# One token granule's second FFN matmul as seven half-size products, with two weight sums on GpSimd

## The chip, the cores and the metric

One NeuronCore of a Trainium2 chip runs the whole program. The metric is device time in microseconds of one execution; three runs of the kernel before gave 208.34, 208.65 and 208.99, with a median of 208.65. A separate, profiled execution gives the trace from which all durations below come.

## The reference

Attention with a local window and a few global keys is followed by a two-layer FFN with a squared ReLU:

```python
scores = scale * np.matmul(q, k.transpose(0, 1, 3, 2))   # q, k, v: (4, 8, 768, 64)
keep = is_global | is_local                               # 8 global keys, 96 local ones
scores = np.where(keep, scores + bias, -1e9)              # bias: -slope * distance
a = softmax(scores)
x = (a @ v).transpose(0, 2, 1, 3).reshape(3072, 512)
h = x @ w_in                                              # (512, 2048)
r = np.maximum(h, 0.0)
out = (s * (r * r) + b) @ w_out                           # (2048, 512), s and b scalars
```

Inputs and output are float32; matmuls run on bfloat16 operands and accumulate in float32.

## The kernel before, in words

Tokens are cut into 12 *granules* of 256 tokens (two blocks of 128), three to a batch; a granule's attention is four *units* of two heads each. For every unit the kernel computes scores on TensorE (`stage_S`, L444), exponentials on ScalarE (L453), a multiplication with a mask template on VectorE (L460), and the product with the values (`stage_A`, L504), whose result VectorE normalizes (a reciprocal L468, a multiplication L469). The granule's normalized rows are transposed into `xT` by DMAs of the SP queue (`x_by_dma`, L612). The first FFN matmul (`p1_mm`, L632) multiplies `xT` with `w_in`, two 128-wide slices of the 2048 at a time; ScalarE takes the ReLU (L642) and VectorE the square (L645), or ScalarE squares four slices at once (L808). The result `gT` holds g = r*r, transposed, for a pair of granules.

The second FFN matmul has two forms. Granules 0 to 3 use the plain one: `p2_mm` (L680) accumulates 16 matmuls of 128x512 for each block of 128 tokens, and VectorE finishes with s and the bias vector `bvec` (`p2_out`, L691; `p2_late`, L713, for the blocks of granules 0 and 1, which were held back until `bvec` existed). Granules 4 to 11 are taken in pairs: a pair's even and odd granule and the halves of the 2048 and of the 512 columns make a 2x2 block product, computed with seven half-size products (`product`, L832) instead of eight. That form needs sums of quarters of g (`g_sum`, L795), sums of the partial results (`scaled` L841, `join` with L880), and four weight matrices that are differences of quarters of `w_out` (w11 and w12 the upper half's left and right columns, w21 and w22 the lower half's): `weight_sums` at L766 to L769, where t1 = w12 - w11, t2 = w22 - t1, t3 = w22 - w12 and t4 = w21 - t2. t3 is written over w12 in the tile `w_out_bf`. Each is one VectorE instruction over 128x2048 elements.

The order of all work is written out by hand: every engine runs its instructions in the order in which the Python code issues them. From granule 4 on, `step(s, c0, c1, c2)` issues, in this order: the scores and exponentials of the next step, the masks of the next step, the list `c0`, `stage_A` of the first unit, a `flush()` of the waiting evacuations (`outs`), `c1`, `stage_A` of the second unit, another flush, and `c2`; at the end of a granule `finish_granule` issues the transposes of `xT` and, on POOL, a one-element copy out of `xT` (the *gate*, L122), behind which the loads of a later granule are queued. Steps 8 to 12 (L1167 to L1176) are the ones that change: they hold the rest of granule 2's and all of granule 3's second matmul, the first matmul of granules 3 and 4, and three of the four weight sums.

PSUM is shared by three pools; the pool `ps_h`, with three banks, serves the FFN of both kinds. SBUF work tiles of one tag and one buffer are reused, so a new user waits for the last reader of the old one.

Of the kernel before, what the change touches and what calls it, by code (L numbers as in the profile page):

```python
# [8 lines left out]
F32 = mybir.dt.float32  # L9
BF16 = mybir.dt.bfloat16  # L10
ACT = mybir.ActivationFunctionType
ALU = mybir.AluOpType
# [5 lines left out]
def kernel(  # L18
# [25 lines left out]
    KC = DM // P  # L44
    FC = DF // P
# [18 lines left out]
    ps_h = ctx.enter_context(tc.tile_pool(name="ps_h", bufs=3, space=bass.MemoryType.PSUM))  # L64
# [102 lines left out]
    s_bc = const.tile([P, 1], F32, name="s_bc")  # L167
    b_bc = const.tile([P, 1], F32, name="b_bc")

    def load_scalars():  # L170
# [23 lines left out]
        out=far, in0=far, scalar=NEG_BIG, in1=rel, op0=ALU.mult, op1=ALU.add  # L194
# [15 lines left out]
    for i in range(2, 4):  # L210
        load_w_in(i, 4)
    nc.gpsimd.affine_select(
        out=late_bf[:, 3, :],
# [411 lines left out]
    def p1_mm(j, fp):  # L625

        g = g_of(j)
        ps = ps_h.tile([P, 2, GT], F32, name="ps_1", tag="psh")
        for i in range(2):
            fc = 2 * fp + i  # L630
            for kc in range(KC):
                nc.tensor.matmul(  # L632
                    ps[:, i, :],
                    lhsT=w_in_bf[:, kc, fc * P : (fc + 1) * P],
                    rhs=xT[j][:, kc, :],
                    start=(kc == 0),
                    stop=(kc == KC - 1),
                )
        gs = g[:, 2 * fp : 2 * fp + 2, :]

        def relu():
            nc.scalar.activation(gs, ps[:], ACT.Relu)  # L642

        def square():
            nc.vector.tensor_tensor(gs, gs, gs, ALU.mult)  # L645

        return relu, square


    bvec = const.tile([P, DM], F32, name="bvec")  # L650
# [24 lines left out]
    def p2_mm(j, tb, lo=0, hi=FC):  # L675
        if lo == 0:
            po_cur[j, tb] = ps_h.tile([P, DM], F32, name="ps_2", tag="psh")
        po = po_cur[j, tb]
        for fc in range(lo, hi):
            nc.tensor.matmul(  # L680
                po[:],
                lhsT=g_of(j)[:, fc, tb * P : (tb + 1) * P],
                rhs=w_out_bf[:, fc, :],
                start=(fc == 0),
                stop=(fc == FC - 1),
            )
# [32 lines left out]
    outs = []  # L719
# [9 lines left out]
    def moe_p2_cols(j, tb, parts):  # L729
# [27 lines left out]
    NH = FC // 2  # L757
    CH = DM // 2
    w11, w12 = (w_out_bf[:, 0:NH, c * CH : (c + 1) * CH] for c in range(2))
    w21, w22 = (w_out_bf[:, NH:FC, c * CH : (c + 1) * CH] for c in range(2))  # L760
    t1, t2, t4 = (
        const.tile([P, NH, CH], BF16, name=f"wsub{i}", tag=f"wsub{i}")[:] for i in range(3)
    )
    t3 = w12
    weight_sums = [
        lambda: nc.vector.tensor_tensor(t1, w12, w11, ALU.subtract),  # L766
        lambda: nc.vector.tensor_tensor(t2, w22, t1, ALU.subtract),
        lambda: nc.vector.tensor_tensor(t3, w22, w12, ALU.subtract),
        lambda: nc.vector.tensor_tensor(t4, w21, t2, ALU.subtract),  # L769
    ]  # L770

    gs_cur = {}
# [5 lines left out]
    def g_sum(pr, n, c=None):  # L778

        def go():  # L780
            if pr not in gs_cur:
                gs_cur[pr] = [
                    gpool.tile([P, NH, GT], BF16, name="gsum", tag=f"gsum{i}", bufs=1)
                    for i in range(4)
                ]
            e, o = 2 * pr, 2 * pr + 1
            cs = slice(0, NH) if c is None else slice(c * NH // 2, (c + 1) * NH // 2)
            s1, s2, s3, s4 = (t[:, cs, :] for t in gs_cur[pr])
            dst, x, y, op = {
                1: (s1, quarter(o, 0, c), quarter(o, 1, c), ALU.add),  # L790
                2: (s2, s1, quarter(e, 0, c), ALU.subtract),
                3: (s3, quarter(e, 0, c), quarter(o, 0, c), ALU.subtract),
                4: (s4, quarter(e, 1, c), s2, ALU.subtract),
            }[n]
            nc.vector.tensor_tensor(dst, x, y, op)  # L795

        return go
# [42 lines left out]
    def scaled(dst, ps, add):  # L840
        nc.vector.scalar_tensor_tensor(  # L841
            out=dst, in0=ps, scalar=s_bc[:], in1=add, op0=ALU.mult, op1=ALU.add
        )

    bdiff = const.tile([P, CH], F32, name="bdiff")
# [33 lines left out]
    def add_f32(dst, x, y):  # L879
        nc.vector.tensor_tensor(dst, x, y, ALU.add)  # L880
# [27 lines left out]
    def join(pr, n):  # L908
# [11 lines left out]

        return go

    def pe(pr, n):

        def go():
            product(pr, n)
            outs.append(lambda: evac(pr, n))

        return go
# [4 lines left out]
    def u1(j, q):  # L934
        return lambda: unit_p1(j, q)

    def late_p1(j, fps):

        def go(fp):
            relu, square = p1_mm(j, fp)  # L940
            relu()
            outs.append(square)

        return [lambda fp=fp: go(fp) for fp in fps]

# [4 lines left out]
    def run(cs):  # L950
        for c in cs:
            c()
# [19 lines left out]
    def step(s, c0, c1, c2, pool=None, pre=()):  # L972

        j = 2 * s // HP
        last = (2 * s + 2) % HP == 0
        if not last and j >= 4 and j + 2 < NJ:
            qk_by_dma(j + 2)
        posts = scores(s + 1)
        exps, masks = [c for i, c in enumerate(posts) if i % 2 == 0], posts[1::2]
        run(exps)  # L980
        run(pre)
        run(masks)
        run(c0)
        stage_A(2 * s)
        flush()
        if not last and j + 1 == QK_PE + 1:
            make_koff(j + 1)
        if not last and j % NGR == 0:
            attach(j // NGR, 1, NB)
        run(c1)  # L990
        stage_A(2 * s + 1, pool)
        flush()
        n = 2 if j < X_PE else 1
        run(c2[0:n])
        if last:
# [167 lines left out]
    def rest(j, tb):  # L1163
        p2_mm(j, tb, FC // 2, FC)
        outs.append(lambda: p2_out(j, tb))

    step(8, [lambda: rest(2, 0)] + late_p1(3, (0,)), late_p1(3, (1, 2)), late_p1(3, (3,)))  # L1167
    step(9, p2[2][1:2], late_p1(3, (4, 5)), late_p1(3, (6, 7)))
    step(10, p2[3][0:1], [lambda: shifted_template(range(H))], late[0:2] + [bias_diff], ps_h)
    step(  # L1170
        11,
        [lambda: p2_mm(3, 1, 0, FC // 2), u1(4, 0)],
        [u1(4, 1)],
        late[2:4] + [shifted_copy, weight_sums[0]],
    )
    step(12, [lambda: rest(3, 1), u1(4, 2)], [weight_sums[1], u1(4, 3)], [weight_sums[2]])  # L1176
    for pr in range(2, NJ // 2):
        e, o = 2 * pr, 2 * pr + 1
        k0 = 2 * e + 5
        if k0 >= NU // 2:  # L1180
            break
        step(
            k0,
            [pe(pr, 2)],
            [u1(o, 0)],
            [u1(o, 1), flush, g_sum(pr, 3, 0)],
            pre=[pe(pr, 1), flush],
        )
        step(
            k0 + 1,  # L1190
            [u1(o, 2)],
            [u1(o, 3), g_sum(pr, 1, 0)],
            [g_sum(pr, 1, 1), pe(pr, 7), g_sum(pr, 2)] + [weight_sums[3]] * (pr == 2),
            pre=[g_sum(pr, 3, 1)],
        )
        tail = k0 + 3 >= NU // 2
        step(
            k0 + 2,
            [u1(e + 2, 0), pe(pr, 5)] if tail else [pe(pr, 5), flush, pe(pr, 6)],
            [pe(pr, 6), g_sum(pr, 4, 0)] if tail else [g_sum(pr, 4, 0), prod(pr, 4)],  # L1200
            [g_sum(pr, 4, 1), u1(e + 2, int(tail)), join(pr, 1)],
        )
# [66 lines left out]
```

The softmax here doesn't subtract the row's maximum and nothing guards it: scores larger than these inputs give would overflow.

## Time and profile before

| | us |
|---|---|
| median of 3 runs | 208.65 (208.34 to 208.99) |
| the profiled execution's own time | 208.38 |
| its span, first to last instruction | 206.6 |
| TensorE busy | 201.9 |
| VectorE busy | 160.9 |
| ScalarE busy | 127.8 |
| GpSimd (POOL) busy | 69.9, nearly all of it issuing DMAs |
| one weight sum on VectorE (L766 to L769) | 1.22 |
| second matmul of granule 3, block 0 (L680) | 76.97 to 80.44 |
| first use of granule 4's `xT` (L632) | 83.20 |

The profile's rows name an engine, a line of the kernel, an operation, what it writes and reads, and a duration. PE is TensorE, DVE VectorE, ACT ScalarE, POOL GpSimd, SP the queue that issues DMAs. Matmul durations overlap, so a stretch of matmuls is read from the start of the first to the start of what follows. POOL was idle from 70.3 to 82.96, waiting for granule 4's `xT`.

### The profile page before, as it was taken

How to read it: one execution, taken by the hardware profiler on the slowest of the kernel's cores; microseconds unless marked ns; L12 is line 12 of the kernel's file. 1: busy time of each engine (PE TensorE's matmuls, PEld its weight loads, DVE VectorE, ACT ScalarE, POOL GpSimd, SP SyncE). 2: the span in 40 equal slices, each digit the busy share in tenths (PEclk: the TensorE clock that was granted, in tenths of full speed). 3: DMA queues.
4: the chain of work that ended last, by engine and by line, in shares of the span. 5: the costliest groups of instructions: out<-in, count | busy, mean ns of one | idle time of the engine just before them, and what ended most of it. 6: DMA issues, size and time to landing. Idle time of an engine off the chain costs nothing.

```text
span 206.6 us, 5313 instructions
## 1 busy us (share of the span) xinstructions
PE 201.9 (98%) x2182; PEld 160.1 (77%) x2190; DVE 160.9 (78%) x338; ACT 127.8 (62%) x197; POOL 69.9 (34%) x90
## 2 busy tenths in 40 slices
PE   8999999999999999999999999999999999999993
PEld 2678884557867585878888898888888889888883
DVE  7977589977989866799799975699866696737974
ACT  5766669486976558685664595663695764476200
POOL 8986333899454500913700907300000000000000
PEclk9999999999999999999999999999999999999999
DMA  5999999999999999999999999999570300240006
GB/s 163 173 179 201 207 206 178 156 153 130 130 147 119 156 121 218 208 195 214 148 205 149 116 125 212 167 219 77 53 206 3 98 9 0 61 145 0 0 10 197
DMA packets 110836, 28.17 MB, mean 136 GB/s; under 512 B 97852, under 2 KB 109308, under 8 KB 110812
## 3 DMA queue, kind: packets, MB, share of 16 engines
q0 software_dynamic: 76000, 13.11, 85.9%
q1 hardware_dynamic: 33612, 14.13, 41.0%
q10 hardware_dynamic: 1200, 0.59, 1.1%
q8 instruction: 17, 0.28, 0.6%
q14 instruction: 7, 0.06, 0.1%
HBM read 27.26 MB, written 6.29 MB: 162 GB/s over the span
## 4 chain that ended last, share of the span: by engine, by line
PE 95%; DMA 2%; DVE 1%; issue 0%; ACT 0%
PE ps L632 41%; PE ps L832 24%; PE ps L680 13%; PE ps_s L444 6%; PE ps_av L504 5%; DMA first<-in_k_dram 2%; PE ps_s L530 1%; PE ps_t L354 1%; PE ps_x L604 1%; PE ps_t L331 1%; PE ps_s L545 1%; PE ps_s L419 1%; PE ps_av L571 1%; PE ps_last L832 0%; PE ps_t L344 0%
## 5 line engine op out<-in xcount | busy, mean ns | idle before, releaser
L632 PE MATMUL ps<-xT,w_in_bf 128*128 128x256 bf16 x768 | 90.4, 273 | 0.1
L642 ACT ACTIVATE gT<-ps 128x512 bf16<-128x512 f32 x96 | 55.9, 598 | 47.9 <-PE ps L632 47.6
L632 PEld LDWEIGHTS <-w_in_bf 128*128 128x128 bf16 x768 | 73.1, 98 | 9.6 <-DVE xT L607 0.2
L453 ACT ACTIVATE pt<-ps_s 128x1024 bf16<-128x1024 f32 (+1 forms) x44 | 39.3, 946 | 3.2 <-PE ps_s L444 3.0
L680 PE MATMUL ps<-w_out_bf,gT 128*128 128x512 bf16 x120 | 28.7, 380 | 0.5 <-issue 0.2
L460 DVE TENSOR_TENSOR pt<-pt,tmpl 128x1024 bf16<-128x1024 bf16 (+1 forms) x40 | 24.4, 643 | 3.8 <-ACT pt L453 3.7
L832 PEld LDWEIGHTS <-gsum 128*128 128x128 bf16 x256 | 24.2, 98 | 3.7 <-DVE gsum L795 0.5
L108 POOL DMA_DIRECT2D vb<-in_v_dram x24 | 21.5, 910 | 5.5 <-DMA w_out_bf<-in_moe_w_out_dram 3.3
L806 DVE TENSOR_TENSOR gT<-gT 128x1024 bf16<-128x1024 bf16 x20 | 13.7, 686 | 11.7 <-ACT gT L642 11.7
L680 PEld LDWEIGHTS <-gT 128*128 128x128 bf16 x128 | 11.7, 98 | 13.0
L469 DVE TENSOR_TENSOR xn<-ps_av,rc 128x256 bf16<-128x256 f32 x48 | 20.4, 424 | 1.7
L832 PEld LDWEIGHTS <-gT 128*128 128x128 bf16 x200 | 18.6, 98 | 2.3
L468 DVE RECIPROCAL rc<-ps_av 128x4 f32<-128x4 f32 x48 | 8.5, 178 | 12.3 <-PE ps_av L504 10.8
L504 PEld LDWEIGHTS <-pt 128*128 128x128 bf16 x320 | 14.4, 97 | 2.7 <-DVE xn L469 0.7
L645 DVE TENSOR_TENSOR gT<-gT 128x512 bf16<-128x512 bf16 x32 | 13.0, 420 | 3.6 <-ACT gT L642 3.3
L504 PE MATMUL ps_av<-vb,pt 128*128 128x65 bf16 x208 | 15.3, 193 | 0.0
L832 PE MATMUL ps<-w_out_bf,gsum 128*128 128x256 bf16 x128 | 15.3, 273 | 0.0
L832 PE MATMUL ps<-wsub,gsum 128*128 128x256 bf16 x128 | 15.1, 273 | 0.0
L116 POOL DMA_DIRECT2D nat<-in_q_dram x14 | 12.4, 888 | 7.0 <-DMA vb<-in_v_dram 2.7
L122 POOL COPY gate<-xT 1x1 bf16<-1x1 bf16 x6 | 1.5, 250 | 37.1 <-DMA xT<-xn 37.1
L116 POOL DMA_DIRECT2D nat<-in_k_dram x14 | 12.4, 884 | 4.9 <-DMA w_in_bf<-in_moe_w_in_dram 2.4
L832 PE MATMUL ps<-w_out_bf,gT 128*128 128x256 bf16 x120 | 13.9, 273 | 0.0
(111 smaller groups left out, 230.5 us busy)
## 6 DMA issues: line engine op xcount, KB each, us to landing
out_dram<-o_q SPq DMA_DIRECT2D x15, 256.0 KB, 2.6
vb<-in_v_dram POOLq DMA_DIRECT2D x24, 128.0 KB, 8.8
nat<-in_k_dram POOLq DMA_DIRECT2D x22, 128.0 KB, 6.7
nat<-in_q_dram POOLq DMA_DIRECT2D x22, 128.0 KB, 6.9
w_out_bf<-in_moe_w_out_dram POOLq DMA_DIRECT2D x4, 512.0 KB, 16.2
w_in_bf<-in_moe_w_in_dram POOLq DMA_DIRECT2D x4, 256.0 KB, 7.5
w_in_bf<-in_moe_w_in_dram POOLq DMA_DIRECT2D x2, 512.0 KB, 11.2
out_dram<-o_sb SPq DMA_DIRECT2D x4, 256.0 KB, 6.1
```

The costliest lines, as they stand in the source:

```text
L108: nc.gpsimd.dma_start(vbuf[b % 2][:, sb, :, 0:D], rows_of(v, b, sb))
L116: nc.gpsimd.dma_start(t[:, n, i, :, :], rows_of(srcs[n], b, sb))
L453: nc.scalar.activation(pt[:, :, 0:ncol], ps[:, :, 0:ncol], ACT.Exp, scale=QSCALE)
L460: nc.vector.tensor_tensor(pv, pv, m.rearrange("p h a c -> p h (a c)"), ALU.mult)
L469: nc.vector.tensor_tensor(dst, av[:, :, :, 0:D], rc[:].to_broadcast((P, 2, 2, D)), ALU.mult)
L504: nc.tensor.matmul(av[:, i, hi, 0 : D + 1], lhsT=pt[:, hi, c * P : (c + 1) * P], rhs=vv, start=(n == 0), stop=(n == len(terms) - 1),)
L632: nc.tensor.matmul(ps[:, i, :], lhsT=w_in_bf[:, kc, fc * P : (fc + 1) * P], rhs=xT[j][:, kc, :], start=(kc == 0), stop=(kc == KC - 1),)
L642: nc.scalar.activation(gs, ps[:], ACT.Relu)
L645: nc.vector.tensor_tensor(gs, gs, gs, ALU.mult)
L680: nc.tensor.matmul(po[:], lhsT=g_of(j)[:, fc, tb * P : (tb + 1) * P], rhs=w_out_bf[:, fc, :], start=(fc == 0), stop=(fc == FC - 1),)
L806: outs.append(lambda: nc.vector.tensor_tensor(gs, gs, gs, ALU.mult))
L832: nc.tensor.matmul(ps[:, tb, cs], lhsT=stat[:, fc, tb * P : (tb + 1) * P], rhs=mov[:, fc, cs], start=(fc == 0), stop=(fc == NH - 1),)
```

## The change

Granule 3's second matmul leaves the plain form. Its two blocks of 128 tokens take the place of a pair's two granules, so that the block product of 2x2 has blocks of 128 tokens, and each of the seven products is eight matmuls of 128x256. The sums of g (`sg_sum`, L943), the products (`sg_prod`, L968), their evacuations and joins are spread over steps 9 to 12. The weight sums are needed earlier, so all four are issued in step 9; the second and the fourth go to GpSimd. Two of granule 3's squares move from VectorE to ScalarE (`act_p1`, L1047). The late blocks of granules 0 and 1 and the copy of the mask template move one to two places back, and the second unit of step 10 uses the pool `ps_av` again.

```diff
     weight_sums = [
         lambda: nc.vector.tensor_tensor(t1, w12, w11, ALU.subtract),
-        lambda: nc.vector.tensor_tensor(t2, w22, t1, ALU.subtract),
+        lambda: nc.gpsimd.tensor_tensor(t2, w22, t1, ALU.subtract),
         lambda: nc.vector.tensor_tensor(t3, w22, w12, ALU.subtract),
-        lambda: nc.vector.tensor_tensor(t4, w21, t2, ALU.subtract),
+        lambda: nc.gpsimd.tensor_tensor(t4, w21, t2, ALU.subtract),
     ]
...
+    def sg_sum(n):
+        def go():
...
+            dst, x, y, op = {
+                1: (sg[1], sg_half(0, 1), sg_half(1, 1), ALU.add),
+                2: (sg[2], sg[1], sg_half(0, 0), ALU.subtract),
+                3: (sg[3], sg_half(0, 0), sg_half(0, 1), ALU.subtract),
+                4: (sg[4], sg_half(1, 0), sg[2], ALU.subtract),
+            }[n]
+            nc.vector.tensor_tensor(dst, x, y, op)
...
+    def sg_prod(n):
+        def go():
...
+            mov = {1: w11, 2: w21, 3: w22, 4: t4, 5: t1, 6: t2, 7: t3}[n]
...
+            for fc in range(NH):
+                nc.tensor.matmul(
+                    ps, lhsT=stat[:, fc, :], rhs=mov[:, fc, :], start=(fc == 0), stop=(fc == NH - 1)
+                )
+            outs.append(lambda: sg_evac(n, ps))
...
+    def act_p1(j, fps):
+        def go(fp):
+            relu, _ = p1_mm(j, fp)
+            relu()
+            gs = g_of(j)[:, 2 * fp : 2 * fp + 2, :]
+            nc.scalar.activation(gs, gs, ACT.Square)
...
-    step(9, p2[2][1:2], late_p1(3, (4, 5)), late_p1(3, (6, 7)))
-    step(10, p2[3][0:1], [lambda: shifted_template(range(H))], late[0:2] + [bias_diff], ps_h)
+    step(
+        9,
+        [weight_sums[0]] + p2[2][1:2] + [weight_sums[1], weight_sums[3]],
+        [sg_sum(3)] + act_p1(3, (4, 5)),
+        late_p1(3, (6,)) + [weight_sums[2]] + late_p1(3, (7,)) + [flush, sg_sum(1)],
+    )
+    step(
+        10,
+        [sg_prod(7), sg_prod(1), sg_prod(2)],
+        [bias_diff, lambda: shifted_template(range(H)), sg_prod(5)],
+        [sg_sum(4)],
+        pre=[sg_sum(2)],
+    )
     step(
         11,
-        [lambda: p2_mm(3, 1, 0, FC // 2), u1(4, 0)],
-        [u1(4, 1)],
-        late[2:4] + [shifted_copy, weight_sums[0]],
+        [sg_prod(6), u1(4, 0)],
+        [sg_join(1), u1(4, 1)],
+        [sg_join(0), sg_join(2), shifted_copy] + late[0:2],
     )
-    step(12, [lambda: rest(3, 1), u1(4, 2)], [weight_sums[1], u1(4, 3)], [weight_sums[2]])
+    step(12, [sg_prod(3), sg_prod(4), u1(4, 2)], [u1(4, 3)], late[2:4])
...
-            [g_sum(pr, 1, 1), pe(pr, 7), g_sum(pr, 2)] + [weight_sums[3]] * (pr == 2),
+            [g_sum(pr, 1, 1), pe(pr, 7), g_sum(pr, 2)],
```

More of the change, by code (lines that the diff above doesn't have):

```diff
@@ L921, in join, with sg_half @@
         return go
+    SG = 3
+    sg = {}
+    def sg_half(half, tb):
+        return g_of(SG)[:, half * NH : (half + 1) * NH, tb * P : (tb + 1) * P]
+    def sg_sum(n):
+        def go():
+            if not sg:
+                for i, key in ((2, (3, 1)), (3, (2, 4))):
+                    t = gpool.tile([P, 2, NH, P], BF16, name="sgsum", tag=f"gsum{i}", bufs=1)
+                    for a, m in enumerate(key):
+                        sg[m] = t[:, a]
+            dst, x, y, op = {
[5 more added lines that the diff above has]
+            nc.vector.tensor_tensor(dst, x, y, op)
+        return go
@@ new lines @@
+    sg_ps = {}
+    sg_r = {}
+    def sg_prod(n):
+        def go():
+            stat = {
+                1: lambda: sg_half(0, 0),
+                2: lambda: sg_half(1, 0),
+                3: lambda: sg[4],
+                4: lambda: sg_half(1, 1),
+                5: lambda: sg[1],
+                6: lambda: sg[2],
+                7: lambda: sg[3],
+            }[n]()
+            mov = {1: w11, 2: w21, 3: w22, 4: t4, 5: t1, 6: t2, 7: t3}[n]
+            bank, c = {1: (0, 0), 7: (0, 1), 2: (1, 0), 5: (2, 0), 6: (4, 0), 3: (3, 0), 4: (3, 1)}[n]
+            if bank not in sg_ps:
+                sg_ps[bank] = ps_h.tile([P, GB, CH], F32, name="ps_2", tag="psh")
+            ps = sg_ps[bank][:, c, :]
+            for fc in range(NH):
[3 more added lines that the diff above has]
+            outs.append(lambda: sg_evac(n, ps))
+        return go
@@ new lines, in sg_store, with sg_evac @@
+    def sg_store(tb):
+        b, g = divmod(SG, NGR)
+        t0 = b * S + g * GT + tb * P
+        nc.sync.dma_start(out[t0 : t0 + P, :], sg_r["out", tb][:])
+    def sg_evac(n, ps):
+        if not sg_r:
+            p0, p1_, p2_ = (
+                work.tile([P, GB, CH], F32, name=f"part{i}", tag=f"part{i}", bufs=1)
+                for i in range(3)
+            )
+            sg_r.update({0: p0[:, 0, :], 6: p0[:, 1, :], 1: p1_[:, 0, :], 7: p2_[:, 0, :]})
+            for tb in range(GB):
+                sg_r["out", tb] = work.tile([P, DM], F32, name="o_sb", tag="o_sb", bufs=3)
+        if n == 1:
+            scaled(sg_r[0], ps, bvec[:, 0:CH])
+        elif n == 2:
+            scaled(sg_r["out", 0][:, 0:CH], ps, sg_r[0])
+        elif n == 5:
+            scaled(sg_r[1], ps, bdiff[:])
+        elif n == 6:
+            scaled(sg_r[6], ps, sg_r[0])
+        elif n == 7:
+            nc.scalar.activation(sg_r[7], ps, ACT.Copy, scale=s_bc[:])
+        elif n == 3:
+            scaled(sg_r["out", 0][:, CH:DM], ps, sg_r[1])
+            sg_store(0)
+        elif n == 4:
+            scaled(sg_r["out", 1][:, 0:CH], ps, sg_r[6])
+            sg_store(1)
@@ L923, in pe, with sg_join, go @@
+    def sg_join(n):
+        def go():
+            if n == 1:
+                add_f32(sg_r[1], sg_r[1], sg_r[6])
+            elif n == 0:
+                add_f32(sg_r[6], sg_r[6], sg_r[7])
+            else:
+                add_f32(sg_r["out", 1][:, CH:DM], sg_r[7], sg_r[1])
+        return go
     def pe(pr, n):
@@ L942, in go @@
             outs.append(square)
+        return [lambda fp=fp: go(fp) for fp in fps]
+    def act_p1(j, fps):
[4 more added lines that the diff above has]
+            nc.scalar.activation(gs, gs, ACT.Square)
         return [lambda fp=fp: go(fp) for fp in fps]
@@ L1167 @@
     step(8, [lambda: rest(2, 0)] + late_p1(3, (0,)), late_p1(3, (1, 2)), late_p1(3, (3,)))
-    step(9, p2[2][1:2], late_p1(3, (4, 5)), late_p1(3, (6, 7)))
-    step(10, p2[3][0:1], [lambda: shifted_template(range(H))], late[0:2] + [bias_diff], ps_h)
+    step(
[10 more added lines that the diff above has]
+        pre=[sg_sum(2)],
+    )
     step(
         11,
-        [lambda: p2_mm(3, 1, 0, FC // 2), u1(4, 0)],
-        [u1(4, 1)],
-        late[2:4] + [shifted_copy, weight_sums[0]],
+        [sg_prod(6), u1(4, 0)],
+        [sg_join(1), u1(4, 1)],
+        [sg_join(0), sg_join(2), shifted_copy] + late[0:2],
     )
-    step(12, [lambda: rest(3, 1), u1(4, 2)], [weight_sums[1], u1(4, 3)], [weight_sums[2]])
+    step(12, [sg_prod(3), sg_prod(4), u1(4, 2)], [u1(4, 3)], late[2:4])
     for pr in range(2, NJ // 2):
```

## The prediction

> **What bounds the kernel now.** I read the busy shares first, then the chain that ended last, then the cost groups of the lines the change touches, then each engine's order of time around 60 to 100 us.
>
> ```profile
> PE 201.9 (98%) x2182; PEld 160.1 (77%) x2190; DVE 160.9 (78%) x338; ACT 127.8 (62%) x197; POOL 69.9 (34%) x90
> ...
> PE 95%; DMA 2%; DVE 1%; issue 0%; ACT 0%
> PE ps L632 41%; PE ps L832 24%; PE ps L680 13%; PE ps_s L444 6%; PE ps_av L504 5%; DMA first<-in_k_dram 2%; PE ps_s L530 1%; PE ps_t L354 1%; PE ps_x L604 1%; PE ps_t L331 1%; PE ps_s L545 1%; PE ps_s L419 1%; PE ps_av L571 1%; PE ps_last L832 0%; PE ps_t L344 0%
> ```
>
> TensorE is the path from start to end, so a microsecond taken from it is a microsecond of time, and so is any wait put on it. In the order of time of TensorE:
>
> ```profile
> 76.97 3.63 PE L680 MATMUL ps<-w_out_bf,gT 128*128 128x512 bf16 x15
> ...
> 83.20 1.91 PE L632 MATMUL ps<-xT,w_in_bf 128*128 128x256 bf16 x16
> ...
> 93.96 3.67 PE L832 MATMUL ps<-w_out_bf,gT 128*128 128x256 bf16 x32
> ```
>
> Columns are start, length, work. The block at 76.97 is the first token block of granule 3 (16 matmuls; one record is missing), and the next work starts at 80.44: 3.47/16 = 216 ns each. Thirty-two 256-wide ones go from 93.96 to 97.57: 112 ns with their first; the chain in order of time has 16 of them in 1.75, 109.4 ns each. TensorE has no gap there.
>
> **What the Trainium skill says.** "SBUF — State Buffer", who interferes with whom: GpSimd reads SBUF through VectorE's second read port; a VectorE instruction with two SBUF inputs and a GpSimd instruction that reads SBUF exclude each other for a whole instruction, first come first served. The trace of before agrees in one direction, twice. The gate copy of one element on POOL takes 0.18 us alone, but:
>
> ```profile
> 82.96 0.47 POOL L122 COPY gate<-xT 1x1 bf16<-1x1 bf16 x1 [12.65 <-DMA xT<-xn]
> 96.24 0.32 POOL L122 COPY gate<-xT 1x1 bf16<-1x1 bf16 x1 [7.46 <-DMA xT<-xn]
> 113.14 0.18 POOL L122 COPY gate<-xT 1x1 bf16<-1x1 bf16 x1 [11.05 <-DMA xT<-xn]
> ...
> 95.30 1.22 DVE L768 TENSOR_TENSOR w_out_bf<-w_out_bf 128x2048 bf16<-128x2048 bf16 x1
> 112.58 0.75 DVE L841 SCALAR_TENSOR_TENSOR part<-ps,s_bc,bdiff 128x512 f32<-128x512 f32 x1
> ```
>
> The second copy ends at 96.56, 0.04 us after L768 ended; the first ends 0.04 us after an L713 (also two SBUF inputs); the third runs under L841, whose first input is in PSUM, and isn't held. In the other direction no POOL arithmetic meets VectorE here, but POOL's DMA instructions do hold VectorE's copies:
>
> ```profile
> 39.99 0.87 POOL L102 DMA_DIRECT2D nat<-in_k_dram  x1
> ...
> 40.39 0.48 DVE L387 COPY ko<-kx 128x64 bf16<-128x64 bf16 x1
> 40.48 0.67 DVE L399 COPY vo<-vb 128x1056 bf16<-128x1056 bf16 x1
> ```
>
> L387's shortest is 0.18 and it ends at 40.87, just as the POOL instruction ends at 40.86. So POOL can hold VectorE nearly to the end of its own instruction.
>
> **The change part by part.** *Removed and added on TensorE:* 32 x 216 ns = 6.92 us go, 56 matmuls of 128x256 x 109.4 ns = 6.12 come: 0.80 us saved.
>
> *Weight sums.* On VectorE one takes 1.22 us (L766 to L769). Two move to POOL; no row shows a POOL tensor_tensor. From below: VectorE's 1.22. From above: "GPSIMD Engine Reference", performance versus the Vector engine, gives 4.497 us for an fp32 add of 2048 elements and about 2.6 cycles an element at 1.2 GHz for two inputs; 16-bit operands may be quicker, I know no reason for much slower: 5.2 is my upper end. I take the page's cycle figure, an estimate of 4.45, since the stated limit counts elements through one port.
>
> *Where they land.* The masks of step 9 end at 71.7 and w12-w11 follows on VectorE to 72.9; t2 starts on POOL at 72.95 and ends at 77.4. VectorE meanwhile runs a reciprocal, a normalization and L691 (PSUM inputs, free of the port) to 74.0. Then the new granule sum (128x1024, 0.69 like L806) has two SBUF inputs: held 3.4 us, to 78.1. The second POOL sum waits for the first's semaphore, so VectorE gets in between; then t4 holds the port from 78.0 to 82.5. Behind the first held sum stands the last normalization of granule 4, ending at 78.5 instead of 75.42. Behind that stands t3 = w22-w12, held to 82.5, done at 83.7.
>
> *Who waits.* TensorE ends its scores at 76.97 and then wants product 7, whose moving operand is t3: idle from 76.9 to 83.8, 6.85 us. VectorE's remaining queue (two squares, two sums, two masks, a normalization) runs 83.7 to 87.5, just ahead of products 1, 2, attention, product 5, attention: no further stall. Net: 6.85 - 0.80 = +6.05 us.
>
> *The clock.* "TensorE: Matmul & The Clock Gate", the HAM clock gate: after an idle window of about 3.4 us the array falls to half clock, and returns after a busy one. The opening shows the half rate: ten 128x512 matmuls take 4.42 us (442 ns against 216). A 6.85 us idle contains such a window wherever it falls. The return costs half of 3.4 to 4.4 us: 1.7 to 2.2, I take 1.95. Bounds: 0 (a short idle) and 3.4 (two windows).
>
> *Side effects costed at nothing.* Two squares go to ACT (L1047, 0.6 each by L642's rate), idle 2.8 us there at 70.9. The removed L691s and two squares relieve VectorE of 2.3 us, the sums and the nine small operations (0.42 each, as L848) return 6.5; from 89 us on VectorE has the room of four removed weight sums, 4.9 us. The SP queue: a store less ahead of the transposes of granule 5, early stores behind them; those transposes wait for their data, in before at 89.2 behind three stores, so they come no later against TensorE. xT of granule 4, issued 3.1 us later, lands at 86.0 (7.4 us as before), and TensorE asks at 89 or later. POOL's gate and the loads of granule 8 behind it move by the same 3.1 us, less than TensorE moves. Without the long stall this cover is gone: xT landed at 82.9 in before, for a use at 83.20, and a TensorE 0.8 us earlier would wait about 0.5 us.
>
> **Sum.** Against the profiled execution (span 206.6, time 208.38): 208.38 + 6.05 + 1.95 = 216.4. The median of the runs is 208.65, 0.27 higher; I say 216.5.
>
> **The rivals.**
> 1. *POOL's sums are short, the port rule holds.* Each us off one sum takes two off the end (t2 and t4 follow each other, t3 waits for both): 3.0 us gives +3.15 and 211.6; under about 4 us the clock may not fall. For it: 16-bit data. Against: the page's count is by element.
> 2. *The port doesn't hold VectorE's two-input operations (not slower).* The sums hide in POOL's idle 12.65 us; t3 is ready at 76.3, ahead of 76.97. TensorE saves 0.80, and xT of granule 4, landing at 82.9 as before, takes 0.5 back: -0.3, 208.35; at best -0.8, 207.85. It decides when a POOL sum holds VectorE under about 1.35 us, at which the stall equals the saving. For it: no trace shows arithmetic on POOL stopping arithmetic on VectorE. Against: the fences above.
> 3. *POOL takes the port twice in a row.* Then the granule sum ends at 82.6, t3 at 84.4, xT is issued at 83.2 and lands at 88.5 to 90.6: 0.7 to 1.5 more, 217.2 to 218.
> 4. *The gate copy behind the sums delays granule 8's loads into its scores.* It costs nothing while t4 ends (82.5) before xT lands (86.0); it needs sums of over 8 us.
>
> **How the numbers follow.** Forecast with its clock fall: 0.58, and its own range 214 to 218.5 (sums of 3.8 to 4.8 us, return of 1.7 to 2.4). Rival 1: 0.16, 209 to 214. Rival 2: 0.18, half of it beyond -0.3%. Rival 3: 0.08. Rival 4: nothing to speak of. The range 209 to 219 leaves out rival 2 and a little on top. About 0.3% (0.6 us) is what a measurement of this kernel tells from no change. Faster 0.09; same 0.10 (the rest of rival 2 and a touch of rival 1); slower 0.81.
>
> **What would show it.** Right: a gap of TensorE of 5 to 7 us before L968's first matmul, ended by L768; a granule sum at L943 of 3 to 4 us, or idle before it; two POOL rows of 4 to 5 us at L767 and L769; half-rate matmuls after the gap. Wrong: POOL rows under 2 us, L943 at 0.7 us right behind L691, no gap at L968. If the gap is there and no matmul after it is slow, the clock step fails alone.

## The result and the profile after

The changed kernel takes 215.97 us (median of six runs, 214.77 to 216.51) against 208.41 for the kernel before (six runs, 208.31 to 208.99): a ratio of 1.0349, 95% interval 1.0315 to 1.0384. It is slower by 7.6 us. The profiled execution took 215.57, with a span of 213.8.

The profile page of the changed kernel, busy shares, the slices of TensorE and of its clock, and the chain that ended last:

```profile
PE 203.6 (95%) x2209; PEld 163.3 (76%) x2214; DVE 168.6 (79%) x345; ACT 129.4 (61%) x200; POOL 77.7 (36%) x92
...
PE   8999999999999944999999999999999999999993
...
PEclk9999999999999995899999999999999999999999
...
PE 85%; DVE 8%; DMA 3%; POOL 1%; issue 1%; POOLq 0%
```

TensorE's busy share falls from 98% to 95%, and its row shows one place for it: slices 15 and 16 of 40 (75 to 86 us). The clock is reduced in slices 16 and 17. VectorE has 8% of the chain, where it had 1%. The order of time on TensorE, columns start, length, work and, in brackets, the idle time before it with what ended it:

```profile
76.83 0.39 PE L444 MATMUL ps_s<-qx,ko 64*128 64x128 bf16 x8
82.85 1.89 PE L968 MATMUL ps<-w_out_bf,sgsum 128*128 128x256 bf16 x8 [5.63 <-DVE w_out_bf L768]
84.53 3.23 PE L968 MATMUL ps<-w_out_bf,gT 128*128 128x256 bf16 x16
87.84 1.03 PE L968 MATMUL ps<-wsub,sgsum 128*128 128x256 bf16 x8
```

TensorE is done with its scores at 77.2 and stands still for 5.63 us ahead of product 7, until t3 (L768) is written. The first products then take twice as long: eight in 1.7 us where the later eight take 0.9. The order of time on VectorE and on POOL shows why t3 was late:

```profile
74.24 3.57 DVE L943 TENSOR_TENSOR sgsum<-gT 128x1024 bf16<-128x1024 bf16 x1
77.73 0.17 DVE L468 RECIPROCAL rc<-ps_av 128x4 f32<-128x4 f32 x1
77.94 0.42 DVE L469 TENSOR_TENSOR xn<-ps_av,rc 128x256 bf16<-128x256 f32 x1
78.28 4.52 DVE L768 TENSOR_TENSOR w_out_bf<-w_out_bf 128x2048 bf16<-128x2048 bf16 x1
...
83.50 0.69 DVE L943 TENSOR_TENSOR sgsum<-gT 128x1024 bf16<-128x1024 bf16 x1
...
73.20 4.06 POOL L767 TENSOR_TENSOR wsub<-w_out_bf,wsub 128x2048 bf16<-128x2048 bf16 x1 [2.67 <-DVE rc L468]
77.33 4.38 POOL L769 TENSOR_TENSOR wsub<-w_out_bf,wsub 128x2048 bf16<-128x2048 bf16 x1
82.96 0.21 POOL L122 COPY gate<-xT 1x1 bf16<-1x1 bf16 x1 [1.25 <-DMA xT<-xn]
```

L943, 0.69 us when nothing is in its way (83.50), takes 3.57 and ends at 77.81, 0.55 after the first POOL sum ended (77.26), which is a little less than its own length: it ran once that sum was over. L768, 1.22 in before, takes 4.52 and ends at 82.80, 1.09 after the second POOL sum (81.71). The second POOL sum is itself 0.32 longer than the first; L943 still ran for 0.48 when it started, which can explain that. The reciprocal and the normalization between them, with PSUM inputs, take their usual 0.17 and 0.42. Windows of 5 us, columns window, length, busy time (and count) of PE, PEld, DVE, ACT, POOL, then the granted clock, DMA share and GB/s:

```profile
80.00:85.00 5.00, 2.15 (x11) 1.53 (x12) 4.93 (x6) 0.00 (x0) 3.39 (x4) 0.54 1.01 128
85.00:90.00 5.00, 5.00 (x56) 3.90 (x55) 3.01 (x8) 2.48 (x10) 3.83 (x5) 0.78 2.02 144
```

A clock of 0.5 in part of each window and 1 in the rest gives these means if the half clock began at 80.4 and ended at 87.2. Matmuls ran under it from 82.85 on, so 4.37 us did the work of 2.19: 2.19 lost.

### The profile page after: what moved, and what is told of

Read it like the earlier page. It is cut to its first block, busy times and chain, and to the rows that moved or that the text cites. A ratio compares the mean times of both kernels' runs of the same rounds, so it can differ in the third digit from the quotient of the medians.

```text
span 213.8 us, 5374 instructions
## 1 busy us (share of the span) xinstructions
PE 203.6 (95%) x2209; PEld 163.3 (76%) x2214; DVE 168.6 (79%) x345; ACT 129.4 (61%) x200; POOL 77.7 (36%) x92
## 4 chain that ended last, share of the span: by engine, by line
PE 85%; DVE 8%; DMA 3%; POOL 1%; issue 1%; POOLq 0%
PE ps L632 37%; PE ps L832 23%; PE ps L680 8%; PE ps_av L504 5%; PE ps_s L444 4%; PE ps L968 4%; DMA vb<-in_v_dram 3%; DVE w_out_bf L768 2%; DVE sgsum L943 2%; POOL nat L102 1%; PE ps_s L530 1%; PE ps_t L354 1%; DVE xn L469 1%; PE ps_x L604 1%; DVE o_sb L691 1%
## 5 line engine op out<-in xcount | busy, mean ns | idle before, releaser
L632 PE MATMUL ps<-xT,w_in_bf 128*128 128x256 bf16 x768 | 90.4, 273 | 0.0
L632 PEld LDWEIGHTS <-w_in_bf 128*128 128x128 bf16 x768 | 73.0, 98 | 9.1 <-DVE xT L607 0.2
L832 PEld LDWEIGHTS <-gsum 128*128 128x128 bf16 x256 | 24.2, 98 | 3.7 <-DVE gsum L795 0.5
L806 DVE TENSOR_TENSOR gT<-gT 128x1024 bf16<-128x1024 bf16 x20 | 13.7, 687 | 11.6 <-ACT gT L642 11.6
L680 PE MATMUL ps<-w_out_bf,gT 128*128 128x512 bf16 x91 | 21.8, 379 | 0.3
L832 PEld LDWEIGHTS <-gT 128*128 128x128 bf16 x200 | 18.6, 98 | 2.3
L504 PEld LDWEIGHTS <-pt 128*128 128x128 bf16 x320 | 14.4, 97 | 2.8 <-DVE xn L469 0.7
L680 PEld LDWEIGHTS <-gT 128*128 128x128 bf16 x96 | 8.9, 98 | 9.6
L504 PE MATMUL ps_av<-vb,pt 128*128 128x65 bf16 x208 | 15.5, 193 | 0.1
L832 PE MATMUL ps<-w_out_bf,gsum 128*128 128x256 bf16 x128 | 15.3, 273 | 0.0
L832 PE MATMUL ps<-wsub,gsum 128*128 128x256 bf16 x128 | 15.1, 273 | 0.0
L645 DVE TENSOR_TENSOR gT<-gT 128x512 bf16<-128x512 bf16 x30 | 12.1, 420 | 3.0 <-ACT gT L642 2.7
L832 PE MATMUL ps<-w_out_bf,gT 128*128 128x256 bf16 x120 | 13.9, 273 | 0.0
L808 ACT ACTIVATE gT<-gT 128x1024 bf16<-128x1024 bf16 x12 | 12.7, 1057 | 0.4
```

The costliest lines, as they stand in the source:

```text
L504: nc.tensor.matmul(av[:, i, hi, 0 : D + 1], lhsT=pt[:, hi, c * P : (c + 1) * P], rhs=vv, start=(n == 0), stop=(n == len(terms) - 1),)
L632: nc.tensor.matmul(ps[:, i, :], lhsT=w_in_bf[:, kc, fc * P : (fc + 1) * P], rhs=xT[j][:, kc, :], start=(kc == 0), stop=(kc == KC - 1),)
L680: nc.tensor.matmul(po[:], lhsT=g_of(j)[:, fc, tb * P : (tb + 1) * P], rhs=w_out_bf[:, fc, :], start=(fc == 0), stop=(fc == FC - 1),)
L806: outs.append(lambda: nc.vector.tensor_tensor(gs, gs, gs, ALU.mult))
L808: nc.scalar.activation(gs, gs, ACT.Square)
L832: nc.tensor.matmul(ps[:, tb, cs], lhsT=stat[:, fc, tb * P : (tb + 1) * P], rhs=mov[:, fc, cs], start=(fc == 0), stop=(fc == NH - 1),)
```

## The experiments

Ten kernels follow. Unless said otherwise, each is the changed kernel with the edit shown. In the kernels that add lines, line numbers move by a few.

**Both POOL sums on VectorE.** Theory: GpSimd's sums cost only because VectorE's operations stand still beside them (the *hold*). Rival: the seven products cost something of their own.

```diff
-        lambda: nc.gpsimd.tensor_tensor(t2, w22, t1, ALU.subtract),
+        lambda: nc.vector.tensor_tensor(t2, w22, t1, ALU.subtract),
...
-        lambda: nc.gpsimd.tensor_tensor(t4, w21, t2, ALU.subtract),
+        lambda: nc.vector.tensor_tensor(t4, w21, t2, ALU.subtract),
```

> The changed kernel with all four weight sums on VectorE, in the same places of the program (the two that were on POOL now stand on VectorE between t1 and the next normalization). Theory (a POOL sum holds VectorE's two-input instructions): no stretched instruction is left, L943 takes 0.7 us and L768 1.2; the two sums add 2.4 us in front of a normalization, which stops TensorE 1.4 us at the attention product and 0.4 at the next first matmul; no gap in front of L968, no clock fall; 209.4 to 210.4. Rival (it is the seven-product form itself, its extra sums or banks, that makes the gap): the gap at L968 stays near 5.7 us, 215 or more.

Measured: 209.84 (209.78 to 209.93), ratio 1.006 (1.0043 to 1.0078). Six of the seven and a half microseconds are gone though VectorE has 2.4 us more to do. Its waits of TensorE, columns engine and line, what it waited for, us in total, times, longest:

```profile
PE ps_av L504 <- DVE xn L469: 1.7, 1, 1.7
...
PE ps L968 <- DVE w_out_bf L768: 0.2, 1, 0.2
```

Three sums in a row stand ahead of a normalization, which makes the 1.7; L943 is back at 0.68. From its scores (78.31) to L832 (95.48) TensorE takes 17.17 us, in before 17.54 (76.42 to 93.96), so the seven products cost it nothing of their own. What remains over before is the two waits, for want of a place for VectorE's sums.

**One sum on POOL.** t2 stays on GpSimd, t4 goes to VectorE, late (product 4 wants it in step 12).

```diff
-        lambda: nc.gpsimd.tensor_tensor(t4, w21, t2, ALU.subtract),
+        lambda: nc.vector.tensor_tensor(t4, w21, t2, ALU.subtract),
...
-        [weight_sums[0]] + p2[2][1:2] + [weight_sums[1], weight_sums[3]],
+        [weight_sums[0]] + p2[2][1:2] + [weight_sums[1]],
...
-        [sg_join(1), u1(4, 1)],
+        [sg_join(1), weight_sums[3], u1(4, 1)],
```

> The changed kernel with the first of the two sums (t2) on POOL as it is, and the second (t4) on VectorE two steps later. Theory: one hold of some 3 us at L943, none at L768, t3 ready at 79.3, gap in front of L968 2.4 us, too short for the clock to fall: 209.6 to 210.6. Rival (the clock falls with any gap, or the gap doesn't go by the number of POOL sums): over 212.

Measured: 211.39 (210.14, 210.59, 212.18, 212.59), ratio 1.0134 (1.0079 to 1.0189). The time was missed at the top, by the clock. Order of time on VectorE and TensorE, and a window (columns as above), profile of the run of 212.59:

```profile
74.25 3.52 DVE L943 TENSOR_TENSOR sgsum<-gT 128x1024 bf16<-128x1024 bf16 x1
...
78.24 1.22 DVE L768 TENSOR_TENSOR w_out_bf<-w_out_bf 128x2048 bf16<-128x2048 bf16 x1
...
79.51 1.05 PE L968 MATMUL ps<-w_out_bf,sgsum 128*128 128x256 bf16 x8 [2.23 <-DVE w_out_bf L768]
```

```profile
80.00:85.00 5.00, 5.00 (x40) 3.85 (x38) 3.44 (x8) 2.06 (x9) 2.87 (x4) 0.66 0.56 97
```

The hold went with the sum, as expected: L943 is held by t2, L768 isn't held by anything, and the gap ahead of L968 is 2.23 us. But this gap was enough for the clock to fall, for 3.4 us (0.66 of 5 us), which costs 1.7. The two runs with a mean clock of 0.998 and 1.0 took 210.59 and 210.14, within the expectation; the two with 0.991 took 212.2 and 212.6.

**The clock kept up.** 24 matmuls without a use fill TensorE's gap.

```diff
-        [sg_prod(7), sg_prod(1), sg_prod(2)],
+        [lambda: warm(24, 4 * P), sg_prod(7), sg_prod(1), sg_prod(2)],
```

> The changed kernel with 24 idle matmuls of 128x512 (5.2 us of TensorE) issued just ahead of product 7, where TensorE waits anyway. Theory (of 7.2 us lost, 2.2 are the half clock after the idle): the gap is filled, the clock stays full, all L968 matmuls take 272 ns, and the time falls by about 2.2 us to 213.4 to 214.2. Rival (the half clock costs nothing, since VectorE sets the pace there): 215.5 to 216.5, unchanged.

Measured: 213.69 (213.24 to 214.14), ratio 1.0245 (1.0219 to 1.0271). Order of time on TensorE:

```profile
77.04 5.42 PE L159 MATMUL ps_w<-const-bfloat16-1.0 128*128 128x512 bf16 x24
82.54 1.05 PE L968 MATMUL ps<-w_out_bf,sgsum 128*128 128x256 bf16 x8
```

The products run at full rate. They start 6.05 us after the first scores (76.49), against 6.25 in the changed kernel (76.60 to 82.85), so hardly any earlier. The half clock after the gap thus cost about 215.97 - 213.69 = 2.3 us, the gap the rest.

**The POOL sums in four pieces each.** If VectorE gets in between pieces, does the hold shrink?

```diff
+    def pool_sum(dst, x, y, n=4):
+        w = NH // n
+        for i in range(n):
+            c = slice(i * w, (i + 1) * w)
+            nc.gpsimd.tensor_tensor(dst[:, c, :], x[:, c, :], y[:, c, :], ALU.subtract)
...
-        lambda: nc.gpsimd.tensor_tensor(t2, w22, t1, ALU.subtract),
+        lambda: pool_sum(t2, w22, t1),
...
-        lambda: nc.gpsimd.tensor_tensor(t4, w21, t2, ALU.subtract),
+        lambda: pool_sum(t4, w21, t2),
```

> The changed kernel with each POOL sum cut into four instructions of 128x512, same work in total. Theory (the port is taken for a whole instruction, and given to the other at its end): each two-input instruction of VectorE waits for at most one piece, about 1.1 us, and POOL's pieces wait for VectorE in turn; L943 and L768 take 1 to 2.5 us, the gap at L968 is 0 to 1.5 us, no clock fall: 209 to 211.5. Rival (POOL keeps the port while it has work queued, or the two share it by the element): gap of 5 us or more, 214 to 216.

Measured: 215.82 (214.76 to 216.83), ratio 1.0347 (1.0298 to 1.0397): a miss, no better than whole sums. Order of time on VectorE, POOL's row of eight pieces, and the longer of two gaps of TensorE:

```profile
74.13 0.68 DVE L949 TENSOR_TENSOR sgsum<-gT 128x1024 bf16<-128x1024 bf16 x1
...
75.47 1.44 DVE L774 TENSOR_TENSOR w_out_bf<-w_out_bf 128x2048 bf16<-128x2048 bf16 x1
76.83 2.67 DVE L645 TENSOR_TENSOR gT<-gT 128x512 bf16<-128x512 bf16 x2
79.53 1.53 DVE L949 TENSOR_TENSOR sgsum<-gT 128x1024 bf16<-128x1024 bf16 x1
81.10 1.52 DVE L949 TENSOR_TENSOR sgsum<-sgsum,gT 128x1024 bf16<-128x1024 bf16 x1
82.54 3.19 DVE L460 TENSOR_TENSOR pt<-pt,tmpl 128x1024 bf16<-128x1024 bf16 x2
...
73.03 12.15 POOL L769 TENSOR_TENSOR wsub<-w_out_bf,wsub 128x512 bf16<-128x512 bf16 x8 [3.85 <-DVE wsub L772]
...
86.34 0.24 PE L504 MATMUL ps_av<-vb,pt 128*128 128x65 bf16 x1 [4.17 <-DVE xn L469]
```

t3 is now in time, and product 7 starts without a gap. But the two engines alternate piece by piece: squares of 0.37 each take 1.3, sums of 0.69 take 1.5, masks of 0.64 take 1.6, until the last piece is through at 85.2. The wait moved: 0.92 us to a product behind a granule sum, and 4.17 to L504, whose normalization stands behind the masks, and the clock fell behind that. The expectation counted one wait each for L943 and L768 (here L949 and L774), and left out that the squares, sums and masks behind them, all with two inputs in SBUF, would each wait for a piece too. The operations shown take 5.7 us more than without a hold, in the changed kernel L943 and L768 took 6.2 more: splitting spreads the hold and hardly lessens it.

**The sums left out.** How much do the seven products save, without sums to hold anything? Products 4 and 6 take t1 in place of t4 and t2, in `product` by the same line, so this kernel's output is a different one, as is that of the next two.

```diff
-            mov = {1: w11, 2: w21, 3: w22, 4: t4, 5: t1, 6: t2, 7: t3}[n]
+            mov = {1: w11, 2: w21, 3: w22, 4: t1, 5: t1, 6: t1, 7: t3}[n]
...
-        [weight_sums[0]] + p2[2][1:2] + [weight_sums[1], weight_sums[3]],
+        [weight_sums[0]] + p2[2][1:2],
```

> The changed kernel without its second and fourth weight sum: products 4 and 6 (of granule 3 and of the later pairs) take t1 in their place, so the output is not the reference's; it shows the seven products of granule 3 without the sums on GpSimd. If the sums are all that costs time, TensorE keeps the 0.80 us that the seven products save, less the wait for granule 4's xT, at most 0.5: 207.6 to 208.2, no gap ahead of L968, L943 at 0.7, full clock. If the finer chain of products, sums and evacuations costs TensorE something of its own, 209 or more.

Measured: 207.84 (207.59 to 208.34, seven runs) against 208.44, ratio 0.9968 (0.9958 to 0.9979): 0.60 us saved. Order of time on TensorE:

```profile
77.13 1.05 PE L968 MATMUL ps<-w_out_bf,sgsum 128*128 128x256 bf16 x8
...
82.71 1.91 PE L632 MATMUL ps<-xT,w_in_bf 128*128 128x256 bf16 x16
...
93.48 3.67 PE L832 MATMUL ps<-w_out_bf,gT 128*128 128x256 bf16 x32
```

From the scores at 76.58 to L832 it is 16.90 us, in before (76.42 to 93.96) 17.54: 0.64 less. POOL's gate copy shows that granule 4's `xT` had landed at 82.63; L632 shows no wait for it. Of the other 0.16 of the 0.80, about 0.1 lies ahead of the second L504 (81.00), which starts just behind the normalization that ends at 80.94; the rest is open.

**GpSimd writes only.** Memsets in the sums' place, two for each, none of which reads SBUF.

```diff
-        lambda: nc.gpsimd.tensor_tensor(t2, w22, t1, ALU.subtract),
+        lambda: [nc.gpsimd.memset(t2, 0.5) for _ in range(2)],
...
-        lambda: nc.gpsimd.tensor_tensor(t4, w21, t2, ALU.subtract),
+        lambda: [nc.gpsimd.memset(t4, 0.5) for _ in range(2)],
```

> The changed kernel with each sum on GpSimd replaced by two memsets of the same tile (128x2048 bf16, a write without a read), so the output is not the reference's. If GpSimd holds VectorE's two-input operations by its reads of SBUF, as the Trainium skill's page "SBUF - State Buffer" says under who interferes with whom, the memsets hold nothing: L943 at 0.7, t3 at 1.2, no gap ahead of L968, and the time of the kernel without the sums, 207.6 to 208.2. If any long GpSimd instruction on SBUF holds VectorE, L943 or t3 is stretched to the end of a memset, and the time is over 209.

Measured: 211.48 (210.7 to 212.28), ratio 1.0131 (1.01 to 1.0162). By the time alone the expectation's second branch would have won. The rows say something else. Order of time on POOL, VectorE and TensorE:

```profile
69.95 3.88 POOL L767 MEMSET wsub<- 128x2048 bf16 x2
73.78 3.94 POOL L769 MEMSET wsub<- 128x2048 bf16 x2
...
69.61 2.48 DVE L399 COPY vo<-vb 128x1056 bf16<-128x1056 bf16 x1
72.13 1.99 DVE L400 COPY vo<-vb 8x1056 bf16<-8x1056 bf16 x1
74.04 1.27 DVE L460 TENSOR_TENSOR pt<-pt,tmpl 128x1024 bf16<-128x1024 bf16 x2
75.24 1.21 DVE L766 TENSOR_TENSOR wsub<-w_out_bf 128x2048 bf16<-128x2048 bf16 x1
...
77.06 0.20 PE L504 MATMUL ps_av<-vb,pt 128*128 128x65 bf16 x1 [2.35 <-DVE xn L469]
```

The memsets start 3 us earlier than the sums did, since nothing makes them wait, and meet other VectorE work. L943 and L768 come after them; the masks and t1, which also have two SBUF inputs, run beside them in 1.27 and 1.21, as in the kernel without the sums. The two copies ahead of them, single-input bf16, are held: 2.48 and 1.99 where that kernel has 0.69 and 0.42. That agrees with the Trainium skill ("SBUF — State Buffer", SBUF: two separate sides), by which a VectorE operation in a two-port mode and any GpSimd operation exclude each other, and one with two SBUF inputs excludes only a GpSimd operation that reads SBUF. That these copies run in a two-port mode is not shown by the trace. The copies' 3.4 us made a gap of 2.35 at L504, with a clock fall in two of the four runs.

**GpSimd reads one input.** Copies in the sums' place.

```diff
-        lambda: nc.gpsimd.tensor_tensor(t2, w22, t1, ALU.subtract),
+        lambda: nc.gpsimd.tensor_copy(t2, t1),
...
-        lambda: nc.gpsimd.tensor_tensor(t4, w21, t2, ALU.subtract),
+        lambda: nc.gpsimd.tensor_copy(t4, t2),
```

> The changed kernel with each sum on GpSimd replaced by a copy of the same 128x2048 elements (t2 from t1, t4 from t2: one input read, where the sum reads two), so the output is not the reference's. If a read on GpSimd is what holds VectorE, L943 and t3 end with a copy's end as they did with a sum's, and the gap ahead of L968 is 5.7 us less two for each us by which a copy is shorter than 4.06 us: for copies of 2 to 4 us a gap of 1.6 to 5.6 us and 209 to 216. If only a sum with two inputs holds it, L943 is 0.7 and the time 207.6 to 208.2.

Measured: 209.26 (209.13 to 209.32), ratio 1.0036 (1.0022 to 1.005). Order of time on POOL, VectorE and TensorE:

```profile
73.09 1.89 POOL L767 COPY wsub<-wsub 128x2048 bf16<-128x2048 bf16 x1 [2.63 <-DVE wsub L766]
75.04 2.23 POOL L769 COPY wsub<-wsub 128x2048 bf16<-128x2048 bf16 x1
...
74.16 1.37 DVE L943 TENSOR_TENSOR sgsum<-gT 128x1024 bf16<-128x1024 bf16 x1
...
76.00 2.36 DVE L768 TENSOR_TENSOR w_out_bf<-w_out_bf 128x2048 bf16<-128x2048 bf16 x1
...
78.41 1.05 PE L968 MATMUL ps<-w_out_bf,sgsum 128*128 128x256 bf16 x8 [1.22 <-DVE w_out_bf L768]
```

L943 and L768 end 0.55 and 1.09 us after the copies (74.98 and 77.27), the very offsets that they had after the sums. So a GpSimd instruction that reads SBUF holds them, with one input or two, and one that only writes does not. The slope of rival 1 held too: a copy is 2.17 us shorter than a sum, which gives a gap of 5.63 - 4.34 = 1.29; measured 1.22, with no clock fall.

**All sums on VectorE, spread.** A version that might beat both. Not shown in the edit: the second and fourth sum go to VectorE as in the first experiment, `step` issues the masks behind the first attention product where `masks_late` is set, and granule 2's two stores go behind granule 4's transposes.

```diff
     step(
         9,
-        [weight_sums[0]] + p2[2][1:2] + [weight_sums[1], weight_sums[3]],
+        [weight_sums[0]] + p2[2][1:2],
         [sg_sum(3)] + act_p1(3, (4, 5)),
-        late_p1(3, (6,)) + [weight_sums[2]] + late_p1(3, (7,)) + [flush, sg_sum(1)],
+        act_p1(3, (6,)) + [weight_sums[2]] + act_p1(3, (7,)) + [weight_sums[1], sg_sum(1)],
     )
...
         pre=[sg_sum(2)],
+        masks_late=True,
...
-        [sg_join(1), u1(4, 1)],
-        [sg_join(0), sg_join(2), shifted_copy] + late[0:2],
+        [sg_join(1), weight_sums[3], u1(4, 1)],
+        [sg_join(0), sg_join(2), shifted_copy],
...
-    step(12, [sg_prod(3), sg_prod(4), u1(4, 2)], [u1(4, 3)], late[2:4])
+    step(12, [sg_prod(3), sg_prod(4), u1(4, 2)], [u1(4, 3)], late[0:2])
...
-            [u1(o, 1), flush, g_sum(pr, 3, 0)],
+            [u1(o, 1), flush, g_sum(pr, 3, 0)] + late[2:4] * (pr == 2),
```

> All seven products with all four weight sums on VectorE, spread so that none stands ahead of a normalization TensorE waits for: t1 first in step 9, t3 and t2 at its end, t4 in step 11; the masks of step 10 behind its first attention product, the four late blocks a step later, and the two stores of granule 2 behind the transposes of granule 4. If the 0.80 us is there to be had and only the places of the sums were in its way: 207.4 to 207.9, faster than before by 0.3 to 0.5%. If VectorE's extra work turns into small waits of TensorE wherever it stands: 208.4 to 209.5.

Measured: 209.81 (209.65 to 209.97), ratio 1.0063 (1.005 to 1.0076): a miss. The waits of TensorE:

```profile
PE ps_av L504 <- DVE xn L469: 1.3, 1, 1.3
...
PE ps L632 <- DVE part L844: 0.7, 1, 0.7
```

Its sums hold nothing, but the masks that I had moved delay the evacuation (here L844) of a product whose bank L632 needs, and the moved late blocks delay a normalization at 106 us. The two, less the 0.60 saved, are 1.4: 209.8.

**The same, its two waits treated.** The edit is against the kernel just shown; `bias_diff` leaves step 10, and `masks_late` counts the masks that go late.

```diff
-        act_p1(3, (6,)) + [weight_sums[2]] + act_p1(3, (7,)) + [weight_sums[1], sg_sum(1)],
+        act_p1(3, (6,)) + [weight_sums[2]] + act_p1(3, (7,)) + [weight_sums[1], bias_diff, sg_sum(1)],
...
-        masks_late=True,
+        masks_late=1,
...
-            [u1(o, 0)],
-            [u1(o, 1), flush, g_sum(pr, 3, 0)] + late[2:4] * (pr == 2),
+            late[2:3] * (pr == 2) + [u1(o, 0)],
+            late[3:4] * (pr == 2) + [u1(o, 1), flush, g_sum(pr, 3, 0)],
```

> As the kernel with all sums spread on VectorE, but with its two waits treated: one of step 10's two masks goes back ahead of the products and bias_diff goes to the idle time of VectorE in step 9 (the wait of 0.67 us ahead of granule 4's first FFN matmul), and the last two late blocks of granule 1 go singly into VectorE's idle times of step 13 (the wait of 1.30 us at 106 us). If those two waits were all that took back the saving, the time is that of the kernel without the sums or a little under: 207.5 to 208.0, faster than before. If VectorE has no room for its 3.8 us of sums and small operations around granule 3, other waits take their place: 208.4 to 209.8.

Measured: 208.25 (208.04 to 208.64, 16 runs) against 208.61, ratio 0.9981 (0.9973 to 0.9989). It beats both kernels, the one before by 0.4 us. That is less than the 0.3% (0.6 us) that the prediction takes one measurement to tell, but with 16 and 20 runs the interval leaves out 1. TensorE's list of waits has none left after the opening. From the scores (76.67) to L832 (93.99; L835 here) it saves 0.22 of the 0.64; waits too short for the list must have taken back the rest, which was not followed further. The time lies between the two expectations.

**The kernel before, with two sums on GpSimd.** One part of the change alone.

```diff
-        lambda: nc.vector.tensor_tensor(t2, w22, t1, ALU.subtract),
+        lambda: nc.gpsimd.tensor_tensor(t2, w22, t1, ALU.subtract),
...
-        lambda: nc.vector.tensor_tensor(t4, w21, t2, ALU.subtract),
+        lambda: nc.gpsimd.tensor_tensor(t4, w21, t2, ALU.subtract),
```

> The kernel before with one part of the change alone: its second and fourth weight sum on GpSimd, at the places that they have there (93 us and 110 us). If the port's hold costs time wherever VectorE's next two-input operation stands ahead of a normalization: t2 (4.1 us) holds L768 about 3 us and t4 (4.1 us) holds the masks of the next step about 3 us, two gaps of TensorE at L504 of 2 to 3 us each, 212 to 215, with up to 2 more if the clock falls. If only the changed kernel's tight place between scores and product 7 made the hold cost anything: 208.3 to 209.5.

Measured: 222.5 (221.98 to 223.31), ratio 1.0662 (1.0641 to 1.0684), far over both. Order of time on POOL, VectorE and TensorE:

```profile
101.62 1.78 POOL L108 DMA_DIRECT2D vb<-in_v_dram  x2
103.38 4.11 POOL L767 TENSOR_TENSOR wsub<-w_out_bf,wsub 128x2048 bf16<-128x2048 bf16 x1
...
100.60 0.68 DVE L806 TENSOR_TENSOR gT<-gT 128x1024 bf16<-128x1024 bf16 x1
102.42 5.63 DVE L806 TENSOR_TENSOR gT<-gT 128x1024 bf16<-128x1024 bf16 x1 [1.14 <-ACT gT L642]
...
111.06 0.24 PE L504 MATMUL ps_av<-vb,pt 128*128 128x65 bf16 x1 [4.92 <-DVE xn L469]
...
124.88 3.57 PE L832 MATMUL ps<-wsub,gT 128*128 128x256 bf16 x16 [4.80 <-POOL wsub L769]
```

What I had left out is POOL's own queue: there the sums stand behind the gate and the loads of a later granule, so t2 starts at 103.4, not 93, and t4 at 120.7, when product 4 already waits for it. And L806, ready at 102.42, ended only at 108.05, 0.56 after t2, though t2's row begins at 103.38 and L806's 0.69 would have fitted ahead of it. What held it for that first microsecond is open. A hold by the load's issue is unlikely: the L806 at 100.60 ran in its usual 0.68 beside such an issue, and of the 33 VectorE operations of this trace that have two bf16 inputs in SBUF and meet POOL's issues alone, none is longer than usual. The two gaps are 9.7 us; each was followed by half clock, with matmuls under it for 5.3 and 5.2 us (half of it lost): 9.7 + 5.2 = 14.9, the difference of the profiled run (223.31) from before.

## Why the prediction was right

The time, the place and the chain of causes were as predicted: 215.97 for 216.5, inside the likeliest case's own range. Its errors of size partly cancel: the gap was put 1.2 us too long, while a saving put 0.2 too large and a half clock put 0.2 too small took 0.4 of that back. Step by step:

| step | predicted | measured |
|---|---|---|
| saving of the seven products | 0.80 | 0.60 (kernel without the sums) |
| one POOL sum | 4.45 | 4.06; the second 4.38 with its own wait |
| first granule sum L943 done | 78.1 | 77.81 |
| last normalization of granule 4 done | 78.5 | 78.36 |
| t3 done | 83.7 | 82.80 |
| TensorE's gap ahead of L968 | 6.85 | 5.63 |
| loss by half clock | 1.95 | 2.19; 2.3 by the filled gap |
| sum, profiled run over before | +8.0 | 5.63 - 0.60 + 2.19 = +7.22; seen 215.57 - 208.38 = +7.19 |

*Weight sums* (the term that was mis-sized): the estimate by elements gave 4.45, a bf16 sum takes 4.06 (4.11 twice in the last experiment). It counts twice, as rival 1 had it, and accounts for 0.8 of the 1.2 us by which the gap came out shorter. The rest is that TensorE came to its wait 0.3 later (77.2 for 76.9) and that t3 ended 1.09 after t4 and not 1.2.

*Where they land*: right, including that VectorE gets in between the two sums; rival 3 did not happen here. It didn't happen between the pieces of the split sum either, which don't depend on each other: the granule sum at 74.13 there ran in its usual 0.68, behind the first and ahead of the second. The last experiment has one operation held for longer than the sum that it met, by a cause that stays open.

*The port*: right, and the write-only and one-input experiments narrow it. It is the read that matters against VectorE's two-input operations. The prediction's evidence for this direction, copies held under POOL's DMA instructions, was of the other kind: in the trace of before, 35 VectorE operations with two bf16 inputs in SBUF meet such an instruction, and none is held. The rule that it cites ahead of them is the one that the sums and copies bear out.

*The clock*: right in size. Its argument that the fall was certain rests on a gap of two windows of 3.4 us; at the measured 5.63 that no longer holds, and the clock still fell in all six runs (mean 0.983 to 0.989). The bound was wrong: under about 4 us, the prediction said, the clock may not fall, and it fell after 2.23, less than the one idle window that it took to be needed. Rival 1's 211.6 for sums of 3.0 us could for that reason have been 1.7 more.

*The saving*: the deduction for `xT` in rival 2 was wrong in its cause. No wait of TensorE for `xT` appears in the kernel without the sums, though the products bring it there earlier (L632 at 82.71, `xT` landed by 82.63); it saved 0.60, between rival 2's two figures of 0.3 and 0.8. One reading under the 0.80 is off: the 32 matmuls that start at 93.96 end where the next work starts, at 97.46 and not 97.57, which gives the 109.4 ns each that the sum uses anyway.

*Side effects*: `xT` of granule 4 was issued at 78.4 and the gate copy ran at 82.96, 4.6 us later, not the 7.4 that I carried over from before, where the SP queue had two stores (L700) between 71.8 and 74.5, just ahead of the transposes. The two spread versions, which issue these stores behind the transposes, speak for a part of it: the gate ran 5.6 us after the issue (75.70 to 81.32 and 75.81 to 81.37), in the kernel without the sums, with the stores ahead, 7.0 (75.61 to 82.63). What made the rest is open. With TensorE at L632 only at 90.4 it made no difference. Rival 4 cost nothing, as said.

## What to carry to other kernels

Work given to an idle GpSimd is not free: in these kernels VectorE's operations with two SBUF inputs stood still until the end of the sum or copy that they met there, and its bf16 copies until the end of a memset; what stands behind them in VectorE's order is late too. Ask where that order meets TensorE before asking how idle GpSimd is; cutting the work into pieces moved the wait and left 5.1 us of the 5.6. A saving of 0.6 us on TensorE leaves room for no wait at all, so each VectorE operation that is added or moved needs a named idle time; with such places, and the other moves of that kernel, the same seven products were worth 0.4 us.

## What the runs showed of the hardware beyond that

- The clock fell after gaps of 5.63, 4.92, 4.80, 4.17, 2.35 and 2.23 us, in the last two only in half of the runs, and not in the profiles with gaps of 1.66, 1.30 and 1.22. In the profiles it stayed at half for 3.41 us (one sum on POOL, memsets) or for 6.83 us (the changed kernel, the split sums and, twice, the last experiment).
- The clock's changes seem to lie on a grid of 3.413 us: in the traces' clock records the full clock lasted 75.09, 78.51 or 105.81 us up to the first fall, which is 22, 23 and 31 times that, and in the last experiment it changed at 109.57, 116.40, 123.22 and 130.05. Whether a gap of 2.2 us lowers the clock would then depend on where in the grid it lies, which would fit its falling in half of the runs; that is argued, not shown.
- On GpSimd 128x2048 bf16 elements took 4.06 us for a sum, 1.89 for a copy and, as the mean of two, 1.94 for a memset.
- A memset, which reads nothing, held VectorE's bf16 copies (2.48 for 0.69) and not its two-input operations.
